# Order of the input loads and the sign step of the weight conversion in a fused retention, channel-mix and gated-MLP kernel on one core

## The chip, the cores and the metric

The kernel runs on one core of a Trainium2 chip. The metric is device time in microseconds, the median of several executions. Names of the engines: PE is TensorE (matmul), PEld its weight loads, DVE is VectorE, ACT is ScalarE, POOL is GpSimd, SP is SyncE, which here only issues DMAs.

## What is computed

Three layers on a batch of 2 with 768 steps and width 512. All arrays come in as float32; the host passes the weight matrices with their bytes viewed as 64-bit words of the kind that the kernel converts (below).

```python
def _attn_ref(q, k, v):                      # 8 heads of 64
    for t in range(S):
        state = gamma * state + einsum('bhd,bhe->bhde', k[:, :, t], v[:, :, t])
        y[:, :, t] = scale * einsum('bhd,bhde->bhe', q[:, :, t], state)

def _moe_ref(x, mu_k, mu_r, w_k, w_v, w_r):  # x_prev is x moved by one step
    xk = mu_k * x + (1.0 - mu_k) * x_prev
    xr = mu_r * x + (1.0 - mu_r) * x_prev
    k = np.maximum(xk @ w_k, 0.0)
    v = k * k @ w_v
    return sigmoid(xr @ w_r) * v

def _moe2_ref(x, w_in, g_ln, w_sg, b_sg, w_out):
    h = gelu_tanh(x @ w_in);  u, v = halves of h
    v_n = (v - mean(v)) / sqrt(var(v) + 1e-6) * g_ln
    v_s = einsum('ts,bsd->btd', w_sg, v_n) + b_sg[None, :, None]
    return x + (u * v_s) @ w_out
```

## The kernel before

**The chunk stage.** The retention runs over 12 chunks of 128 steps, numbered 0 to 11, the two batches in turn. A chunk has two loads of 512 KB each, `chunk<-qk` (queries and keys) and `chunk<-kv` (keys and values by token); I call them qk4, kv4 and so on. Its work on PE is `sc` (scores, L410), `y` from the state (L472, not for chunks 0 and 1), `st` (the state's update, L446, not for the last two chunks) and `y` from the scores (L483). POOL scales the values (`vs`, L424; for chunks 0 and 1 DVE does it), DVE masks the scores (`prs`, two operations to a chunk, L419) and, when both batches of a step range are through, scales `y` into `x` (two operations, L497). The state is copied from PSUM to `scr` by ACT or DVE (L241).

**The dense stage.** The rest are dense products of a 128-row weight block with 512 columns, each done as three passes (high part by high part, high by low, low by high) on fp32r pairs, 12 or 24 matmuls of 128x512 to an output tile, all issued at L322. Columns are in 3 blocks of 512. The order is: `kp` (x by w_k, 8 tiles) of block 0, a few `kp` tiles of block 1 ahead of time (EARLY of them), `rp` (w_r) and `vp` (w_v) of block 0, the same for blocks 1 and 2, then the MLP (`vp` and `up` by w_in, `sp` by w_sg, `op` by w_out). The input of a `kp` or `rp` product is made on DVE and ACT: `mix` (L521, L527), then the pair `xo` (a cast, and a subtraction at L311).

**Weights.** A weight piece (512 KB) is loaded into one of three `raw` buffers as 64-bit words. `convert` makes an fp32 value from two 32-bit halves: ACT scales the upper word (L267), ACT or DVE prepares the lower one (L275, L278), DVE joins them (L282, L285), DVE puts the sign bit in (L289), one of both casts the high part, and DVE subtracts for the low part (L293). There are 32 such pieces: 8 of w_k, 4 of w_r, 8 of w_v, 8 of w_in, 4 of w_out. The `kp` tile m needs w_k piece m.

**What sets the order.** The program builds a list of operations with costs, and `Plan.order` plays them through with a little model of the engines and of the DMA link; the order in which it starts them is the order of instructions on every engine. Pools limit it: `p4` has 17 slots, of which up to CHUNKS may hold chunk halves; `raw` has 3; `t` has 8 + EARLY. The chip then only waits for data, buffers and the landing of the DMA that is eight places earlier in SP's queue. All loads go through SP, in its order. w_k loads are let in once kv1 has landed in the model (`after=` in `raw_load`).

Of the kernel before, what the change touches and what calls it, by code (L numbers as in the profile page):

```python
# [35 lines left out]
WARM_UP = 10  # L36
EARLY = 5
CHUNKS = 6
XO = 4
DMA_SCRATCH = 4096  # L40
V_ON_POOL = tuple(range(2, 12))
LINK = 0.1
SLACK = {"raw": 2.0}
DMA_LEAD = 1.9
DMA_RATE = 0.40
F64_SIGN = -(1 << 31)
F64_REBIAS = 2.0 ** -112
# [4 lines left out]
class Plan:  # L52
# [28 lines left out]
    def order(self):  # L81
# [16 lines left out]
        engines = ("PE", "DVE", "ACT", "POOL", "SP")  # L98
        idle = {e: 0.0 for e in engines}
        queue = {e: [] for e in engines}  # L100
        seq, events, link = [], [(0.0, -1, e) for e in engines], 0.0
        started = [False] * n
# [30 lines left out]
        def start(i, t, eng):  # L133
# [14 lines left out]
            if eng == "SP":  # L148
                busy = t + 0.1
                link = max(t + DMA_LEAD, link + cost / DMA_RATE) if cost else link  # L150
                done = max(t + DMA_LEAD, link)
            else:
                busy = done = t + cost
# [43 lines left out]
def fused_kernel(ctx, tc, qk, kv, w_k, w_v, w_r, w_in, w_sg, w_out, consts, ydec, b_sg, out):  # L197
# [48 lines left out]
    def raw_load(key, src, dt, mb):  # L246
        buf = ("raw", key)
        plan.op("SP", mb, lambda: sp.dma_start(out=T[buf], in_=src), w=[(buf, 0)],
                new=[new("raw", "raw", buf, (128, src.shape[-1]), dt)],
                after=plan.writer[("kv", 1), 0])  # L250
        return buf

    def convert(name, j, src, dst, tag, part, first):
# [4 lines left out]
        def word(k):  # L258
            return T[raw].bitcast(I32).rearrange("p (n two) -> p n two", two=2)[:, :, k]

        def xf():
            return T[xb]

        def xi():
            return T[xb].bitcast(I32)

        plan.op("ACT", .68, lambda: act.activation(out=xf(), in_=word(1).bitcast(F32), func=ACTF.Copy,  # L267
                                                   scale=F64_REBIAS),
                r=[(raw, 0)], w=[(xb, 0)], new=[new_t("cv", xb)])
# [10 lines left out]
        def join():  # L280
# [7 lines left out]
        plan.op("DVE", .69, join, r=[(raw, 1)], w=[(xb, 0)])  # L288
        plan.op("DVE", .69, lambda: dve.scalar_tensor_tensor(  # L289
            out=xi(), in0=word(1), scalar=F64_SIGN, in1=xi(), op0=ALU.bitwise_and, op1=ALU.bitwise_or),  # L290
            r=[(raw, 0)], w=[(xb, 0)])
        cast(lambda: dst(T[wb][0]), lambda: T[xb], [(xb, 0)], [(wb, ("hi", part))], [first] if first else [])
# [544 lines left out]
```

## Time and profile before

| | before |
|---|---|
| median of 3 runs | 367.78 us (364.86 to 370.07) |
| profiled execution, its time | 369.48 us |
| span of the instructions in it | 367.4 us |
| PE busy | 354.3 us (96%) |
| DVE busy | 246.6 us (67%) |
| ACT busy | 155.4 us (42%) |
| POOL busy | 17.4 us (5%) |
| moved from and to HBM | 35.97 MB |

Times inside the profile count from the first instruction. The profiled execution took 2.1 us more than its span. A busy share is an average over stages: the shares of DVE and ACT are much higher in the first 120 us than later.

### The profile page before, as it was taken

How to read it: one execution, taken by the hardware profiler on the slowest of the kernel's cores; microseconds unless marked ns; L12 is line 12 of the kernel's file. 1: busy time of each engine (PE TensorE's matmuls, PEld its weight loads, DVE VectorE, ACT ScalarE, POOL GpSimd, SP SyncE). 2: the span in 40 equal slices, each digit the busy share in tenths (PEclk: the TensorE clock that was granted, in tenths of full speed). 3: DMA queues.
4: the chain of work that ended last, by engine and by line, in shares of the span. 5: the costliest groups of instructions: out<-in, count | busy, mean ns of one | idle time of the engine just before them, and what ended most of it. 6: DMA issues, size and time to landing. Idle time of an engine off the chain costs nothing.

```text
span 367.4 us, 5406 instructions
## 1 busy us (share of the span) xinstructions
PE 354.3 (96%) x2154; PEld 295.1 (80%) x2154; DVE 246.6 (67%) x481; ACT 155.4 (42%) x264; POOL 17.4 (5%) x19
## 2 busy tenths in 40 slices
PE   5959999999999999999999999999999999999995
PEld 2848888888888888888888888888888888899884
DVE  2779999899899895025899448669384666436422
ACT  1147538988998773006897034324133000000000
POOL 0334510000000000000000000000000000000000
PEclk9969999999999999999999999999999999999999
DMA  7999626114464025000133101110211000110032
GB/s 257 414 409 407 276 59 189 40 59 144 146 197 145 0 64 167 0 0 2 57 114 116 44 0 45 43 43 2 49 38 45 0 0 2 52 62 2 29 115 86
DMA packets 12136, 35.97 MB, mean 98 GB/s; under 512 B 1232, under 2 KB 3408, under 8 KB 12112
## 3 DMA queue, kind: packets, MB, share of 16 engines
q1 hardware_dynamic: 12112, 35.63, 28.6%
q8 instruction: 17, 0.28, 0.3%
q14 instruction: 7, 0.06, 0.1%
HBM read 32.48 MB, written 3.15 MB: 97 GB/s over the span
## 4 chain that ended last, share of the span: by engine, by line
PE 86%; DMA 7%; DVE 5%; SPq 1%; issue 0%
PE vp L322 27%; PE kp L322 18%; PE sp L322 14%; PE up L322 9%; PE rp L322 9%; PE op L322 7%; DMA chunk<-qk 3%; DMA scr<-ydec 2%; DVE prs L419 2%; DMA out<-o 2%; PE sc L410 1%; PE y L483 1%; DVE xo L311 1%; DVE o L732 1%; DVE mix L527 1%; DVE x L497 1%
## 5 line engine op out<-in xcount | busy, mean ns | idle before, releaser
L322 PE MATMUL kp<-xo,wk 128*128 128x512 f32 x288 | 66.5, 390 | 0.0
L322 PE MATMUL vp<-k,wv 128*128 128x512 f32 x288 | 65.8, 389 | 0.0
L322 PEld LDWEIGHTS kp<-xo,wk 128*128 128x128 f32 x288 | 53.8, 188 | 11.6 <-issue 0.5
L322 PEld LDWEIGHTS vp<-k,wv 128*128 128x128 f32 x288 | 54.1, 188 | 11.2
L322 PE MATMUL sp<-wsg,vh 128*128 128x512 f32 (+1 forms) x288 | 50.2, 336 | 0.0
L322 PEld LDWEIGHTS sp<-wsg,vh 128*128 128x128 f32 x288 | 44.4, 190 | 5.7
L322 PE MATMUL vp<-win,x2o 128*128 128x512 f32 x144 | 33.1, 389 | 0.0
L322 PE MATMUL up<-x2o,win 128*128 128x512 f32 x144 | 33.1, 389 | 0.0
L322 PE MATMUL rp<-xo,wr 128*128 128x512 f32 x144 | 33.1, 389 | 0.0
L322 PE MATMUL op<-gt,wout 128*128 128x512 f32 x144 | 33.0, 389 | 0.0
L322 PEld LDWEIGHTS vp<-win,x2o 128*128 128x128 f32 x144 | 27.0, 188 | 5.6
L322 PEld LDWEIGHTS up<-x2o,win 128*128 128x128 f32 x144 | 27.0, 188 | 5.6
L322 PEld LDWEIGHTS rp<-xo,wr 128*128 128x128 f32 x144 | 27.0, 188 | 5.6
L322 PEld LDWEIGHTS op<-gt,wout 128*128 128x128 f32 x144 | 27.0, 188 | 5.6
L566 DVE TENSOR_TENSOR x<-vp,x 128x512 f32<-128x512 f32 x12 | 8.3, 692 | 27.9 <-PE vp L322 27.9
L710 DVE SCALAR_TENSOR_TENSOR g<-sp,con,bsg 128x512 f32<-128x512 f32 x12 | 9.0, 752 | 23.4 <-PE sp L322 23.4
L267 ACT ACTIVATE cv<-raw 128x512 f32<-128x512 f32 x32 | 20.9, 668 | 6.5 <-DMA raw<-w_k 6.1
L289 DVE SCALAR_TENSOR_TENSOR cv<-raw,cv 128x512 int32<-128x512 int32 x32 | 22.1, 691 | 0.8
L547 ACT ACTIVATE k<-rk 128x512 fp32r<-128x512 f32 x19 | 12.0, 631 | 24.5 <-DVE rk L541 24.1
L732 DVE TENSOR_TENSOR o<-op,x 128x256 f32<-128x256 f32 (+1 forms) x20 | 8.8, 474 | 19.8 <-PE op L322 13.7
L410 PE MATMUL sc<-chunk 64*128 64x128 f32 x192 | 14.6, 296 | 7.8 <-DMA chunk<-qk 7.8
L410 PEld LDWEIGHTS sc<-chunk 64*128 64x128 f32 x192 | 12.4, 199 | 10.2 <-issue 6.1
(82 smaller groups left out, 416.9 us busy)
## 6 DMA issues: line engine op xcount, KB each, us to landing
chunk<-qk SPq DMA_DIRECT2D x12, 512.0 KB, 9.8
chunk<-kv SPq DMA_DIRECT2D x12, 512.0 KB, 10.1
raw<-w_k SPq DMA_DIRECT2D x8, 512.0 KB, 8.5
raw<-w_v SPq DMA_DIRECT2D x8, 512.0 KB, 3.5
raw<-w_in SPq DMA_DIRECT2D x8, 512.0 KB, 4.0
out<-o SPq DMA_DIRECT2D x12, 256.0 KB, 2.2
raw<-w_sg SPq DMA_DIRECT2D x6, 384.0 KB, 3.2
raw<-w_r SPq DMA_DIRECT2D x4, 512.0 KB, 4.1
```

The costliest lines, as they stand in the source:

```text
L267: plan.op("ACT", .68, lambda: act.activation(out=xf(), in_=word(1).bitcast(F32), func=ACTF.Copy, scale=F64_REBIAS), r=[(raw, 0)], w=[(xb, ...
L289: plan.op("DVE", .69, lambda: dve.scalar_tensor_tensor(out=xi(), in0=word(1), scalar=F64_SIGN, in1=xi(), op0=ALU.bitwise_and, op1=ALU.bitw ...
L311: plan.op("DVE", .69, lambda: dve.tensor_tensor(out=lo(), in0=src(), in1=hi(), op=ALU.subtract), r=[*keep, (buf, ("hi", part))], w=[(buf, ...
L322: pe.matmul(out=T[ps][:, cols], lhsT=l(), rhs=r(), start=first and q == 0 and i == 0, stop=q == 2 and i == len(grp) - 1, skip_group_check= ...
L410: pe.matmul(out=T["sc", i, p][:, j * CH:(j + 1) * CH], lhsT=a[par[p], 1, j], rhs=a[par[p], 0, j], start=j == 0, stop=j == KD - 1, skip_gro ...
L419: plan.op("DVE", .66, lambda p=p: dve.tensor_tensor(out=T["pr", i % 4][:, p], in0=heads(T["sc", i, p]), in1=T["mask"].unsqueeze(1).to_broa ...
L483: pe.matmul(out=y_at(i, j, p), lhsT=T["vs", i][:, 2 * j + p], rhs=T["pr", i % 4][:, p, j], start=c == 0 and b == 0 and j < 2, stop=b == B ...
L497: dve.tensor_tensor(out=T[x][:, e::2, :, 1 + off:1 + off + CH], in0=T["y", c, e].rearrange("p (b j t) -> p j b t", b=B, t=CH), in1=table[: ...
L547: plan.op("ACT", .63, lambda: act.activation(out=T[o][:, 0], in_=T[rk], func=ACTF.Square), r=[(rk, 0)], w=[(o, ("hi", 0))], new=[new_p("k2 ...
L566: plan.op("DVE", .69, lambda: dve.tensor_tensor(out=T[x2][:, m], in0=T[ps], in1=T[x2][:, m], op=ALU.mult), r=[(ps, 0)], w=[(x2, m)])
L710: dve.scalar_tensor_tensor(out=out_, in0=in_, scalar=T["vec"][:, 2, m:m + 1], in1=t.unsqueeze(1).to_broadcast([128, B, BW]) if last else t ...
L732: plan.op("DVE", .69 if g == B else .42, lambda n=n, ps=ps, o=o, m=m, part=part, of=of: dve.tensor_tensor(out=T[o][:, part], in0=T[ps][:, ...
```

## The change

Constants: eight chunk buffers for six, six early `kp` tiles for five (and so one more slot in `t`), and other numbers in the planner's model (start time, issue time, lead, tail and rate of the link). The w_k loads are let in two at a time, after the kv loads of chunks 4, 5, 6 and 7. In `convert` ACT's scaling uses Prelu with a negative scale and a slope of 2^-32 in place of Copy: a negative value comes out larger by 2^32 than a positive one of the same size, so that a bit of its exponent stands where the left shift by 3 in the join turns it into the sign; the DVE instruction that put in the sign bit is gone.

```diff
--- before.py
+++ after.py
@@ -34,16 +34,20 @@
 RSQRT_SEED = float(0x5F3759DF)
 PIECE = 512
 WARM_UP = 10
-EARLY = 5
-CHUNKS = 6
+EARLY = 6
+CHUNKS = 8
 XO = 4
+WK_AFTER = {("wk", j): k for j, k in enumerate((4, 4, 5, 5, 6, 6, 7, 7))}
 DMA_SCRATCH = 4096
 V_ON_POOL = tuple(range(2, 12))
 LINK = 0.1
 SLACK = {"raw": 2.0}
-DMA_LEAD = 1.9
-DMA_RATE = 0.40
-F64_SIGN = -(1 << 31)
+BEGIN = 0.75
+ISSUE = 0.4
+DMA_LEAD = 1.4
+DMA_TAIL = 2.0
+DMA_RATE = 0.41
+F64_SIGN = 2.0 ** 32
 F64_REBIAS = 2.0 ** -112
 F64_LOW_SCALE = 2.0 ** -29 * (1 - 2.0 ** -20)
 F64_LOW_BIAS = -0.4999
@@ -96,9 +100,9 @@
         home = {}
         pending = {}
         engines = ("PE", "DVE", "ACT", "POOL", "SP")
-        idle = {e: 0.0 for e in engines}
+        idle = {e: BEGIN for e in engines}
         queue = {e: [] for e in engines}
-        seq, events, link = [], [(0.0, -1, e) for e in engines], 0.0
+        seq, events, link = [], [(BEGIN, -1, e) for e in engines], 0.0
         started = [False] * n
 
         def put(i):
@@ -146,9 +150,10 @@
                 home[buf] = (pool, kind)
                 wait[pool].remove((i, kind))
             if eng == "SP":
-                busy = t + 0.1
-                link = max(t + DMA_LEAD, link + cost / DMA_RATE) if cost else link
-                done = max(t + DMA_LEAD, link)
+                busy = t + ISSUE
+                late = link > t + DMA_LEAD + 1.0
+                link = max(t + DMA_LEAD, link) + cost / DMA_RATE
+                done = link + (DMA_TAIL if late else 0.8)
             else:
                 busy = done = t + cost
             idle[eng] = busy
@@ -247,7 +252,7 @@
         buf = ("raw", key)
         plan.op("SP", mb, lambda: sp.dma_start(out=T[buf], in_=src), w=[(buf, 0)],
                 new=[new("raw", "raw", buf, (128, src.shape[-1]), dt)],
-                after=plan.writer[("kv", 1), 0])
+                after=plan.writer[("kv", WK_AFTER.get(key, 1)), 0])
         return buf
 
     def convert(name, j, src, dst, tag, part, first):
@@ -264,8 +269,8 @@
         def xi():
             return T[xb].bitcast(I32)
 
-        plan.op("ACT", .68, lambda: act.activation(out=xf(), in_=word(1).bitcast(F32), func=ACTF.Copy,
-                                                   scale=F64_REBIAS),
+        plan.op("ACT", .68, lambda: act.activation(out=xf(), in_=word(1).bitcast(F32), func=ACTF.Prelu,
+                                                   scale=-F64_REBIAS * F64_SIGN, alpha=1.0 / F64_SIGN),
                 r=[(raw, 0)], w=[(xb, 0)], new=[new_t("cv", xb)])
         by = []
 
@@ -286,9 +291,6 @@
                                          op1=ALU.bitwise_or)
         plan.op("DVE ACT", (.42, .68), lower, r=[(raw, 0)], w=[(raw, 1), (xb, 0)])
         plan.op("DVE", .69, join, r=[(raw, 1)], w=[(xb, 0)])
-        plan.op("DVE", .69, lambda: dve.scalar_tensor_tensor(
-            out=xi(), in0=word(1), scalar=F64_SIGN, in1=xi(), op0=ALU.bitwise_and, op1=ALU.bitwise_or),
-            r=[(raw, 0)], w=[(xb, 0)])
         cast(lambda: dst(T[wb][0]), lambda: T[xb], [(xb, 0)], [(wb, ("hi", part))], [first] if first else [])
         plan.op("DVE", .69, lambda: dve.tensor_tensor(out=dst(T[wb][1]), in0=T[xb], in1=dst(T[wb][0]),
                                                       op=ALU.subtract),
```

The lines of the changed kernel are two to five higher than before (PE's L322 is L324, the loads at L248 are L253, the join at L282 is L287).

SP's queue from the load of qk3 on, before. `raw` is a weight buffer, `chunk` a chunk half, and the number tells the buffer: chunk_150 is qk3, chunk_168 kv3, chunk_274 kv5.

```order
L351 DMA chunk_150<-qk 128x1024
L248 DMA raw_152<-w_k 128x512
L248 DMA raw_155<-w_k 128x512
L248 DMA raw_157<-w_k 128x512
L354 DMA chunk_168<-kv 128x1024
L351 DMA chunk_216<-qk 128x1024
L354 DMA chunk_240<-kv 128x1024
L351 DMA chunk_262<-qk 128x1024
L354 DMA chunk_274<-kv 128x1024
```

The same place in the changed kernel, where chunk_149 is qk3, chunk_152 kv3 and chunk_290 qk7.

```order
L353 DMA chunk_149<-qk 128x1024
L356 DMA chunk_152<-kv 128x1024
L353 DMA chunk_154<-qk 128x1024
L356 DMA chunk_179<-kv 128x1024
L353 DMA chunk_212<-qk 128x1024
L356 DMA chunk_228<-kv 128x1024
L353 DMA chunk_260<-qk 128x1024
L356 DMA chunk_271<-kv 128x1024
L353 DMA chunk_290<-qk 128x1024
L253 DMA raw_294<-w_k 128x512
L253 DMA raw_296<-w_k 128x512
L253 DMA raw_324<-w_k 128x512
```

kv3 now follows qk3 at once; the first three w_k loads moved from behind qk3 to behind qk7. The other five stand behind kv11, where before three of them stood among the chunk loads.

PE's queue at the end of the chunk stage, before: chunks 8 to 11 (x8 is one chunk's worth of matmuls).

```order
L472 MATMUL y<-chunk,scr_119 64x128 x8
L322 MATMUL kp<-xo,wk_284 128x512 x4
L410 MATMUL sc<-chunk 128x128 x8
L472 MATMUL y<-chunk,scr_119 64x128 x8
L446 MATMUL st<-vs,chunk 64x64 x8
L483 MATMUL y<-prs_147,vs 64x128 x8
L446 MATMUL st<-vs,chunk 64x64 x8
L483 MATMUL y<-prs_147,vs 64x128 x8
L410 MATMUL sc<-chunk 128x128 x16
L472 MATMUL y<-chunk,scr_118 64x128 x16
L322 MATMUL kp<-xo,wk_284 128x512 x4
L483 MATMUL y<-prs_148,vs 64x128 x16
```

And the same place in the changed kernel.

```order
L474 MATMUL y<-chunk,scr_129 64x128 x8
L412 MATMUL sc<-chunk 128x128 x8
L474 MATMUL y<-chunk,scr_129 64x128 x8
L448 MATMUL st<-vs,chunk 64x64 x8
L485 MATMUL y<-prs_137,vs 64x128 x8
L448 MATMUL st<-vs,chunk 64x64 x8
L485 MATMUL y<-prs_137,vs 64x128 x8
L412 MATMUL sc<-chunk 128x128 x16
L474 MATMUL y<-chunk,scr_128 64x128 x16
L324 MATMUL kp<-xo,wk_526 128x512 x4
L485 MATMUL y<-prs_138,vs 64x128 x16
```

Of the two groups of four `kp` matmuls that stood ahead of the last `y` one has moved behind it.

DVE's queue in the chunk stage, before, from the scores of chunk 3 to those of chunk 5; L282 is the join of a w_k piece, L289 its sign, L293 its low part.

```order
L419 TENSOR_TENSOR prs_148<-sc,con 128x512 x2
L282 SCALAR_TENSOR_TENSOR cv<-cv,raw 128x512
L289 SCALAR_TENSOR_TENSOR cv<-raw,cv 128x512
L282 SCALAR_TENSOR_TENSOR cv<-cv,raw 128x512
L289 SCALAR_TENSOR_TENSOR cv<-raw,cv 128x512
L293 TENSOR_TENSOR wk_285<-cv,wk_284 128x512
L282 SCALAR_TENSOR_TENSOR cv<-cv,raw 128x512
L293 TENSOR_TENSOR wk_285<-cv,wk_284 128x512
L419 TENSOR_TENSOR prs_147<-sc,con 128x512 x2
L289 SCALAR_TENSOR_TENSOR cv<-raw,cv 128x512
L497 TENSOR_TENSOR x<-y,scr_119 128x2x2x128 x2
L419 TENSOR_TENSOR prs_147<-sc,con 128x512 x2
```

And in the changed kernel, from the scores of chunk 3 to the first join (L287).

```order
L421 TENSOR_TENSOR prs_138<-sc,con 128x512 x2
L246 COPY scr_129<-st 128x512
L499 TENSOR_TENSOR x<-y,scr_129 128x2x2x128 x2
L421 TENSOR_TENSOR prs_137<-sc,con 128x512 x4
L529 SCALAR_TENSOR_TENSOR mix<-x,con,mix 128x512 x3
L499 TENSOR_TENSOR x<-y,scr_128 128x2x2x128 x2
L505 COPY x<-x 128x8
L421 TENSOR_TENSOR prs_138<-sc,con 128x512 x4
L313 TENSOR_TENSOR xo<-mix,xo 128x512 x3
L529 SCALAR_TENSOR_TENSOR mix<-x,con,mix 128x512
L287 SCALAR_TENSOR_TENSOR cv<-cv,raw 128x512
```

The joins moved from ahead of chunk 4's scores to behind chunk 7's, and no sign instruction is left between them.

Counted over the whole program DVE has 470 instructions for 483 (32 sign steps fewer, 19 others taken over from ACT), ACT 247 for 266 with three table loads in each, PE the same 1814 rows.

## Rows read from the trace of the kernel before

**Rows 1.** Who TensorE waited for, whole span: total us, times, longest

```profile
PE sc L410 <- DMA chunk<-qk: 7.8, 3, 4.1
```

**Rows 2.** The chain that ended last: start us, length us, what

```profile
51.05 1.12 PE kp L322 x4
52.17 1.94 PE y L483 x32
54.11 33.79 PE kp L322 x148
...
363.65 0.68 DVE o L732
```

**Rows 3.** Busy us (instructions) by stretch, granted clock, DMA share, GB/s

```profile
20.00:30.00 10.00, 7.11 (x96) 6.17 (x96) 7.66 (x11) 5.53 (x10) 4.41 (x4) 0.66 1.03 409
50.00:120.00 70.00, 70.00 (x359) 57.85 (x356) 64.64 (x106) 60.16 (x104) 0.00 (x0) 1.00 0.42 128
```

**Rows 4.** Timeline: start us, length us, engine; in brackets idle time and releaser

```profile
16.12 0.67 ACT L267 ACTIVATE cv<-raw 128x512 f32<-128x512 f32 x1 [1.32 <-DMA raw<-w_k]
...
19.09 0.66 ACT L267 ACTIVATE cv<-raw 128x512 f32<-128x512 f32 x1 [1.72 <-DMA raw<-w_k]
...
21.55 1.09 POOL L424 TENSOR_TENSOR vs<-chunk,con 128x512 f32<-128x512 f32 x1 [6.90 <-DMA chunk<-kv]
...
22.89 2.08 PE L410 MATMUL sc<-chunk 64*128 64x128 f32 x16 [4.07 <-DMA chunk<-qk]
...
24.11 1.18 POOL L424 TENSOR_TENSOR vs<-chunk,con 128x512 f32<-128x512 f32 x1 [1.47 <-DMA chunk<-kv]
...
26.67 1.09 POOL L424 TENSOR_TENSOR vs<-chunk,con 128x512 f32<-128x512 f32 x1 [1.38 <-DMA chunk<-kv]
```

**Rows 5.** Timeline, TensorE pieces of the chunk stage

```profile
9.12 1.16 PE L410 MATMUL sc<-chunk 64*128 64x128 f32 x16 [3.11 <-DMA chunk<-qk]
...
25.80 1.92 PE L483 MATMUL y<-prs,vs 128*64 128x128 f32 x16
...
28.36 1.16 PE L410 MATMUL sc<-chunk 64*128 64x128 f32 x16
...
30.05 0.69 PE L446 MATMUL st<-vs,chunk 128*64 128x64 f32 x16
...
32.88 1.16 PE L410 MATMUL sc<-chunk 64*128 64x128 f32 x16
...
36.26 0.69 PE L446 MATMUL st<-vs,chunk 128*64 128x64 f32 x16
```

**Rows 6.** Timeline, VectorE operations of the chunk stage

```profile
8.38 1.28 DVE L419 TENSOR_TENSOR prs<-sc,con 128x512 f32<-128x512 f32 x2
...
21.66 1.53 DVE L293 TENSOR_TENSOR wk<-cv,wk 128x512 fp32r<-128x512 f32 x1
...
23.71 0.68 DVE L293 TENSOR_TENSOR wk<-cv,wk 128x512 fp32r<-128x512 f32 x1
...
30.76 2.85 DVE L527 SCALAR_TENSOR_TENSOR mix<-x,con,mix 128x512 f32<-128x512 f32 x3
...
33.54 1.28 DVE L497 TENSOR_TENSOR x<-y,scr 128x512 f32<-128x512 f32 x2
...
38.67 1.74 DVE L311 TENSOR_TENSOR xo<-mix,xo 128x512 fp32r<-128x512 f32 x2
```

**Rows 7.** Page, groups of instructions: count, busy us, mean ns, idle before

```profile
L267 ACT ACTIVATE cv<-raw 128x512 f32<-128x512 f32 x32 | 20.9, 668 | 6.5 <-DMA raw<-w_k 6.1
L289 DVE SCALAR_TENSOR_TENSOR cv<-raw,cv 128x512 int32<-128x512 int32 x32 | 22.1, 691 | 0.8
L547 ACT ACTIVATE k<-rk 128x512 fp32r<-128x512 f32 x19 | 12.0, 631 | 24.5 <-DVE rk L541 24.1
```

**Rows 8.** Page, DMA issues: count, size, median us to landing

```profile
raw<-w_v SPq DMA_DIRECT2D x8, 512.0 KB, 3.5
```

## The prediction

> **What bounds the kernel now.** I read the chain of work that ended last first. From 54.11 us on it is TensorE's dense products, one behind the other, until only the last output tile is left [rows 2], and of all that TensorE waited for in the whole span, the one long item is `sc` for a chunk's qk load: 7.8 us in three waits, the longest 4.1 [rows 1]. All three lie in the chunk stage. So the time is the start of the unbroken dense stream, 54.11, plus what comes behind it, 367.40 - 54.11 = 313.29 us, which no instruction of this change makes shorter. The question is only how early the stream can start, and whether it stays fed.
>
> Why it starts at 54.11 is told by the timeline around 20 us. ACT gets the first w_k piece at 16.1 and the second at 19.1; POOL gets kv3 at 21.5, TensorE qk4 at 22.9, POOL kv4 at 24.1 and kv5 at 26.7 [rows 4]. Between kv4 and kv5 one more load lands, so a load of 512 KB takes 2.56 / 2 = 1.28 us of the link, and they land in the order of SP's queue: three w_k pieces stand there between qk3 and kv3. TensorE, through with chunk 2 at 22.89 - 4.07 = 18.8, idles for qk4. Behind that idle time its granted clock falls: 0.66 in the mean over 20 to 30 us [rows 3], with `sc` at 2.08 us for 1.16 and a `y` at 1.92 [rows 4, 5]. From the `sc` of chunk 5, 28.36, TensorE and VectorE then work almost without a pause.
>
> **The change part by part. The queue.** Each load is equally large, so I take a landing time as a slot and put the new order into the old slots. kv3 now has the slot of the first w_k piece, 16.1, and qk4 that of the second, 19.1. From there at 1.28 us each: qk5 is two loads later, 21.6; qk8 is eleven later (with three w_k pieces ahead of kv7), 33.2; kv11 is eighteen later, 42.1. The 2.97 us between the first two pieces, in place of 1.28, is a hiccup that I leave where it was.
>
> **TensorE's sum.** Until 18.8 I change nothing: `st` and `y` of chunk 0 now stand ahead of `sc` of chunk 1, and wait for `prs`, 8.38 + 1.28 = 9.66 [rows 6]; the `sc` that was done at 10.3 is done about 1.5 us later, but the stage then waits for qk2 in both orders. The prices at full clock: two `sc` with the two `y` from the state take 36.26 - 32.88 = 3.38, so 1.69 for a chunk; two `st` with their `y` take 32.88 - 30.05 = 2.83, so 1.415 [rows 5]; the last two `y` take 1.94, a group of four `kp` 1.12 [rows 2]. With kv3 and qk4 there in time, `st` and `y` of chunk 3 end at 18.8 + 1.4 = 20.2, and the `sc` of chunk 5 starts near 21.5 in place of 28.36. What is left from 20.2: 8 x 1.69 + 6 x 1.415 + 1.94 + 1.12 = 25.1, which ends at 45.3. But `sc` of chunk 8 is reached after 4 x 1.69 + 3 x 1.415 = 11.0, at 31.2, and qk8 lands at 33.2: a new stall of 2.0, and the end is **47.3**.
>
> **VectorE's sum.** It must not be later. From the end of chunk 3's `y`, 20.2, to the last `prs` its new order holds four pairs of `x` and eight of `prs` (12 x 1.28 = 15.4), four `mix` at 2.85 / 3 = 0.95 (3.8), four `xo` subtractions at 1.74 / 2 = 0.87 (3.5), two joins at 0.69 (1.4), one low part of w_k between 0.68 and 1.53 (1.1), and short copies (0.3) [rows 6, 7]: 25.5, so 45.7, and one `y` more, 46.7. The two engines are as good as level, and hand work to each other in turn. I add 0.6 us for that, my choice, with 0 and 2.5 as its ends: the stream starts at **47.9**.
>
> One group of four `kp` fewer is done ahead of the last `y`, so 1.12 us comes back behind it. The sum is 47.9 + 1.12 + 313.29 = 362.3 for the span, 5.1 less than 367.4.
>
> **The sign step.** 32 x 0.691 = 22.1 us of DVE work go [rows 7]. Two of them would lie in the sum above; the rest lies beside the dense stream, where TensorE waits for nothing, and is worth nothing by itself. If that cover were gone, it would be worth at most the 0.69 of a piece that is waited for. The planner gives DVE 19 other instructions from ACT, so both get lighter. A `raw` buffer comes free one DVE step earlier. **Prelu** is in no trace here. Below, the cheapest one-pass ACT row of this shape is 0.631, above, two passes of the Copy are 1.34; I take the Copy's 0.668, since it is one instruction on the same operands [rows 7].
>
> The Trainium skill, ScalarE: Activation LUTs (Step-by-step: what each stage is for), says that an ACTIVATE's cost per element is the same whatever the function; Copy and Square here, 0.668 and 0.631, agree but for a few per cent. By that rule Prelu changes nothing; it is one reason why I give its rival below little.
>
> **The weights behind the queue.** Five w_k pieces now stand behind kv11. The first of them needs a `raw` buffer, free at the first join (20.2 + 15 us of VectorE's list, about 36), and lands a slot behind kv11, at 43.4; `kp` tile 3 wants it at 47.9 + 1.8 + 2 x 2.74 = 55 (12 matmuls at 33.79 / 148 each [rows 2]). The sixth piece waits for the third join, which stands behind the last `prs`, so about 47; an unloaded link brings it in 3.5 [rows 8], and three ACT steps, one join and their turn make it about 57, wanted at 60.5. The last two follow with as much room. So I cost the move at nothing; its cover is some 3 us, and each us beyond that would be a us of stall. Six early tiles, a bigger `t` pool and the new planner numbers add no instruction to the path. The end of the program is in the same order as before.
>
> **Against which time.** On the profiled execution's own 369.48 the sum gives 364.4. The median of the runs shown, 367.78, is 1.7 lower, and with it the sum gives 362.7. I cannot tell whether the median execution had the hiccup and the slow clock in full, so I lean to the median without taking all of it: 363.2, about 1.3% less. A measurement of this kernel can tell about 2% from no change.
>
> **The rivals.**
>
> *The stream starves (0.15).* ACT was busy 60.2 and DVE 64.6 of the 70 us from 50 to 120 [rows 3]; a stream that starts 5 us earlier wants w_k, `xo` of block 1, w_r and w_v earlier. For it: these shares. Against it: both engines get lighter, and TensorE did not wait once there. It would give the gain back and end at 366 to 368.
>
> *The slow clock comes elsewhere (0.10).* An idle 3.11 us ahead of `sc` at 9.12 left that piece at 1.16 us, 4.07 did not leave the next at that [rows 4, 5]; the new order idles some 2.5 us at 6, and 2.0 at chunk 8. A half-clock stretch lengthens one `sc` and one `y` by 0.9 us each, and `st` and others by a few tenths: 2.2 us. Time 365.4.
> The Trainium skill, TensorE: Matmul & The Clock Gate (Part 1: The HAM clock gate), says that the throttled state is the default, that activity releases it, and that the moment varies from run to run; the rows agree with the first part, no run here shows the second.
>
> *Everything falls well (0.17).* No hiccup (TensorE's sum 1.7 shorter: 45.6), hand-offs free, low prices on VectorE (four `xo` and a low part at 0.68: 1.2 less, so 45.5): the stream starts at 45.6, 7.4 less than before with the 1.12 paid back. That gives 360.4, at the edge of 2%.
>
> *Slower (0.04).* Prelu is dear. ACT has 70 - 60.2 = 9.8 us to spare from 50 to 120, and converts 17 pieces there. At two passes that is 17 x 0.67 = 11.4 more, a stall of 1.6: 364.8. It decides from 375.1 on, 12 above my time: (12 + 9.8) / 17 = 1.28 us more for each, a Prelu of 1.95 us.
>
> **How the numbers follow.** The forecast has 0.54. Its own range is 47.3 to 49.8 for the start, on either base: 362 to 366. For 8 in 10 the range takes in the starved and slow-clock cases and half of the good one, 360.0 to 367.0. Faster by over 2% means under 360.4: the good case's better part, and a little from the forecast for the spread of the runs, 0.17 in all. Slower takes the last rival, 0.04. Within 2% is the rest, 0.79.
>
> **What would show it.** Right: TensorE's wait for qk4 gone, `sc` of chunk 5 at 21 to 22, no stretch of half clock near 21 to 28, a wait of 1 to 3 us at chunk 8 near 31, the dense stream unbroken from 47 to 50 on, the L272 group at 0.67 us. Wrong: a dense stream that starts by 50 but has waits for `wk`, `xo` or `wv` behind it (starved), `prs` as the releaser of many `y` (VectorE bound, hand-offs mis-sized), a granted clock under 1 in another stretch, or an L272 of over 1 us.

## The result

The changed kernel takes **362.86 us** (median of 4 runs, 362.21 to 364.01) where the kernel before takes 368.15 (4 runs, 364.86 to 370.07): a ratio of 0.987, with a 95% interval of 0.983 to 0.991. That is 1.3% faster, and so within 2%; the forecast was 363.2. The profiled execution took 363.22, with a span of 361.4. Of the ten runs of e5 below two (369.94, the profiled one, and 370.14) lie more than 1.5% above its fastest and are left out of its median, and the start of its stream is not given.

| | before | forecast | after |
|---|---|---|---|
| start of the unbroken dense stream, us | 54.11 | 47.9 | 47.25 |
| what comes behind it, to the end of the span | 313.3 | 314.4 | 314.2 |
| `sc` of chunk 5 | 28.36 | 21.5 | 21.5 |
| TensorE's waits for qk | 7.8 in three | 2.0 at chunk 8 | 1.0 at chunk 8 |
| first ACT step of a weight piece (32 of them) | 0.668 | 0.668 | 0.667 |

What comes behind is the span less the start: 361.4 - 47.25 = 314.2. First TensorE's waits over the whole span of the changed kernel (who waited for whom: total us, times, longest); it answers to [rows 1].

```profile
PE st L448 <- DVE vs L430: 1.7, 1, 1.7
PE warm L390 <- DVE x L494: 1.2, 1, 1.2
PE sc L412 <- DMA chunk<-qk: 1.0, 1, 1.0
PE y L474 <- ACT scr L246: 0.5, 1, 0.5
```

Of the three waits for qk one of 1.0 us is left. The list is complete: nothing in it is a `kp`, `rp` or `vp`, so the dense stream is not interrupted. Its chain (start us, length us, what) says the same, and answers to [rows 2]. It also shows what ended last ahead of the stream: VectorE's last `prs`.

```profile
43.72 2.40 DVE prs L421 x4
46.11 0.04 issue
46.16 1.09 PE y L485 x14
47.25 37.43 PE kp L324 x164
84.68 10.88 PE rp L324 x48
```

Then the stretches (us, and for PE, PEld, DVE, ACT and POOL the busy us with their instructions; granted clock, DMA share, GB/s), which answer to [rows 3].

```profile
0.00:20.00 20.00, 17.10 (x228) 12.55 (x230) 8.23 (x16) 1.87 (x2) 5.20 (x9) 0.91 0.90 346
20.00:30.00 10.00, 10.00 (x222) 9.07 (x220) 10.00 (x17) 7.43 (x13) 4.73 (x5) 1.00 1.03 408
30.00:40.00 10.00, 8.47 (x172) 7.40 (x169) 10.00 (x14) 4.94 (x9) 6.18 (x5) 1.00 1.01 399
40.00:50.00 10.00, 9.95 (x124) 8.03 (x121) 10.00 (x16) 5.46 (x10) 1.51 (x2) 1.00 0.37 112
50.00:120.00 70.00, 70.00 (x310) 57.95 (x310) 59.51 (x101) 56.38 (x99) 0.00 (x0) 1.00 0.41 130
```

The granted clock is 1.00 from 20 to 30 us, where it was 0.66. VectorE is busy 10.00 of 10 us in each of the three stretches of the chunk stage: it, not TensorE (8.47 from 30 to 40), is now the fuller engine there. From 50 to 120 it went from 64.64 to 59.51 busy, ACT from 60.16 to 56.38. One stretch of slower clock is new, early on (0.91 from 0 to 20). It is seen in TensorE's timeline (start us, length us, engine, operation; in brackets the idle time ahead and who ended it):

```profile
8.97 2.56 PE L485 MATMUL y<-prs,vs 128*64 128x128 f32 x16
...
11.47 2.39 PE L412 MATMUL sc<-chunk 64*128 64x128 f32 x32
...
20.47 2.06 PE L412 MATMUL sc<-chunk 64*128 64x128 f32 x32
...
31.93 1.16 PE L412 MATMUL sc<-chunk 64*128 64x128 f32 x16 [1.03 <-DMA chunk<-qk]
```

Sixteen `y` take 2.56 us at 8.97, where 1.05 is usual, and 32 `sc` take 2.39 at 11.47 for 2.06 at 20.47. The slow stretch took the place of the wait for qk2 that the forecast had there (the list above has none), and so hardly moved anything: the `y` of chunk 2 ended at 19.2, and 18.8 had been forecast.

The weight group of the profile's page, which answers to the first of [rows 7] (count, busy us, mean ns, idle before):

```profile
L272 ACT ACTIVATE cv<-raw 128x512 f32<-128x512 f32 x32 | 20.9, 667 | 0.0
```

### The profile page after: what moved, and what is told of

Read it like the earlier page. It is cut to its first block, busy times and chain, and to the rows that moved or that the text cites. A ratio compares the mean times of both kernels' runs of the same rounds, so it can differ in the third digit from the quotient of the medians.

```text
span 361.4 us, 5364 instructions
## 1 busy us (share of the span) xinstructions
PE 353.2 (98%) x2154; PEld 294.4 (81%) x2154; DVE 232.9 (64%) x468; ACT 143.3 (40%) x245; POOL 17.6 (5%) x19
## 3 DMA queue, kind: packets, MB, share of 16 engines
HBM read 32.48 MB, written 3.15 MB: 99 GB/s over the span
## 4 chain that ended last, share of the span: by engine, by line
PE 86%; DMA 10%; DVE 2%; issue 0%; SPq 0%
PE vp L324 27%; PE kp L324 18%; PE sp L324 14%; PE op L324 9%; PE up L324 9%; PE rp L324 9%; DMA chunk<-kv 4%; DMA raw<-w_k 3%; DMA chunk<-qk 3%; DVE prs L421 1%; DVE cv L287 0%; PE y L485 0%; DVE wk L295 0%; DVE x L499 0%; DVE o L734 0%
## 5 line engine op out<-in xcount | busy, mean ns | idle before, releaser
L324 PE MATMUL kp<-xo,wk 128*128 128x512 f32 x288 | 66.2, 390 | 0.0
L324 PE MATMUL vp<-k,wv 128*128 128x512 f32 x288 | 65.8, 389 | 0.0
L324 PEld LDWEIGHTS kp<-xo,wk 128*128 128x128 f32 x288 | 53.9, 188 | 11.5 <-issue 0.3
L324 PEld LDWEIGHTS vp<-k,wv 128*128 128x128 f32 x288 | 54.1, 188 | 11.2
L324 PE MATMUL sp<-wsg,vh 128*128 128x512 f32 (+1 forms) x288 | 50.2, 336 | 0.0
L324 PEld LDWEIGHTS sp<-wsg,vh 128*128 128x128 f32 x288 | 44.4, 190 | 5.7
L324 PE MATMUL rp<-xo,wr 128*128 128x512 f32 x144 | 33.1, 389 | 0.0
L324 PE MATMUL vp<-win,x2o 128*128 128x512 f32 x144 | 33.1, 389 | 0.0
L324 PE MATMUL up<-x2o,win 128*128 128x512 f32 x144 | 33.1, 389 | 0.0
L324 PE MATMUL op<-gt,wout 128*128 128x512 f32 x144 | 33.0, 389 | 0.0
L324 PEld LDWEIGHTS rp<-xo,wr 128*128 128x128 f32 x144 | 27.0, 188 | 5.6
L324 PEld LDWEIGHTS vp<-win,x2o 128*128 128x128 f32 x144 | 27.0, 188 | 5.6
L324 PEld LDWEIGHTS up<-x2o,win 128*128 128x128 f32 x144 | 27.0, 188 | 5.6
L324 PEld LDWEIGHTS op<-gt,wout 128*128 128x128 f32 x144 | 27.0, 188 | 5.6
L287 DVE SCALAR_TENSOR_TENSOR cv<-cv,raw 128x512 int32<-128x512 int32 x23 | 17.4, 758 | 1.3 <-ACT raw L280 1.3
L529 DVE SCALAR_TENSOR_TENSOR mix<-x,con,mix 128x512 f32<-128x512 f32 x24 | 18.1, 777 | 0.1
L552 DVE TENSOR_TENSOR k<-rk,k 128x512 fp32r<-128x512 f32 x18 | 12.4, 688 | 8.5 <-ACT rk L551 8.5
```

The lines of the kernel that those rows point to most:

```text
L287: dve.scalar_tensor_tensor(out=xi(), in0=xi(), scalar=3, in1=word(0), op0=ALU.logical_shift_left, op1=ALU.bitwise_or)
L324: pe.matmul(out=T[ps][:, cols], lhsT=l(), rhs=r(), start=first and q == 0 and i == 0, stop=q == 2 and i == len(grp) - 1, skip_group_check= ...
L529: plan.op("DVE", .75, lambda: dve.scalar_tensor_tensor(out=seg(T[f]), in0=T[x][:, kk, :, 1:BW + 1], scalar=T["vec"][:, i, kk:kk + 1], in1= ...
L552: plan.op("DVE", .69, lambda: dve.tensor_tensor(out=T[o][:, 1], in0=T[rk], in1=T[o][:, 0], op=ALU.subtract), r=[(rk, 0), (o, ("hi", 0))], ...
```

## The experiments

The theory after the result was the prediction's: the load order and the buffers that let it be (the **loads** half) bring the gain, and the shorter conversion (the **Prelu** half) lies under the dense stream and is worth little. The rival: VectorE has so little to spare behind an earlier stream that without the Prelu half the gain is lost. A third view gave part of the gain to the planner's new numbers. Ratios below are against the kernel before in the same session (its medians there: 368.14, 368.30 and 368.29). They are the record's, and not always the quotient of the two medians: for e7 that would be 0.985. The changed kernel was run in the first session alone, four times.

| kernel | median us (runs) | ratio, 95% | stream starts |
|---|---|---|---|
| the changed kernel | 362.86 (4) | 0.987, 0.983 to 0.991 | 47.25 |
| e1: after, with the sign step | 367.87 (10) | 0.999, 0.996 to 1.003 | 51.9 |
| e2: before, with Prelu alone | 366.75 (10) | 0.996, 0.993 to 1.000 | 51.08 |
| e3: before, with the loads alone | 367.22 (10) | 1.000, 0.996 to 1.003 | 47.01 |
| e10: before, with both, old planner | 362.76 (4) | 0.987, 0.981 to 0.994 | 45.84 |
| e8: after, sign step for w_k only | 366.18 (10) | 0.995, 0.992 to 0.998 | 46.44 |
| e9: after, sign step for the others | 363.81 (10) | 0.991, 0.987 to 0.994 | 47.17 |
| e4: after, w_k let in from the start | 364.26 (10) | 0.991, 0.987 to 0.994 | 48.65 |
| e5: after, six chunk buffers | 364.66 (8) | 0.992, 0.988 to 0.996 | |
| e7: after, w_k let in by chunks 7 to 10 | 362.71 (4) | 0.983, 0.979 to 0.987 | 47.47 |
| e12: e10, w_k spread over chunks 5 to 10 | 362.78 (6) | 0.987, 0.983 to 0.992 | 46.08 |
| e13: after, the same spread | 362.36 (6) | 0.987, 0.983 to 0.991 | 46.69 |
| e11: after, `vs` on ACT | 364.87 (10) | 0.994, 0.991 to 0.997 | 45.68 |

Most of these orders put one group of four `kp` (1.1 us) ahead of the start of the stream; before, e2 and e7 have two there, and e11 has none. Starts are to be compared with that in mind.

### The two halves apart

**e1**: the changed kernel with the conversion of before; the sign step stands inside the planner's entry of the join, so the order of all else is held.

```diff
-  func=ACTF.Prelu, scale=-F64_REBIAS * F64_SIGN, alpha=1.0 / F64_SIGN),
+  func=ACTF.Copy, scale=F64_REBIAS),
...
   # in join, behind its own instruction
+  dve.scalar_tensor_tensor(out=xi(), in0=word(1), scalar=F64_SIGN, in1=xi(),
+                           op0=ALU.bitwise_and, op1=ALU.bitwise_or)
```

> The changed kernel with Copy and the sign step back in the conversion, its order of all other instructions held as the changed kernel has it. Theory (the load order brings the gain, VectorE is full from 20 to 46 us of the chunk stage and free of consequence later): two sign steps lie ahead of the last prs, at 0.69 to 1.53 us each as the join there takes, so the dense stream starts 1.4 to 3.1 later than 47.25 and the time is 364.3 to 366.0; the 30 others cost nothing, TensorE waits for nothing behind 50 us. Rival A (the lighter conversion brings most of the gain): the time goes back to 367 to 368. Rival B (a raw buffer that is free one step earlier feeds the dense stream): waits of TensorE for wk, wr or wv behind 50 us.

Measured: 367.87, and the whole gain is gone: the time of rival A, with the waits of rival B. This is the miss that matters. TensorE's waits in e1 (as above; lines two on):

```profile
PE y L487 <- issue: 1.9, 1, 1.9
PE kp L326 <- DVE xo L246: 1.4, 1, 1.4
...
PE vp L326 <- ACT wv L246: 1.0, 1, 1.0
```

There are now 2.4 us of waits in the dense stream, for `xo` and for a converted piece of w_v. The stretches of e1, the first of them the 24 us from the start of its stream on, and then the same 24 us of the changed kernel:

```profile
51.91:75.91 24.00, 22.59 (x99) 18.42 (x99) 23.70 (x40) 19.58 (x35) 0.00 (x0) 1.00 0.42 132
50.00:120.00 70.00, 67.52 (x317) 55.18 (x313) 68.97 (x116) 54.78 (x96) 0.00 (x0) 1.00 0.42 129
```

```profile
47.25:71.25 24.00, 24.00 (x106) 19.85 (x107) 22.21 (x38) 21.69 (x39) 0.00 (x0) 1.00 0.41 132
```

VectorE is busy 23.70 of the 24 us for 22.21, and 68.97 of 70 from 50 to 120: it has next to nothing left. TensorE loses 2.5 us from 50 to 120, and ACT does 19.58 us of work in the 24 where the changed kernel's did 21.69. The profiled execution was a long one, 371.20: of its later start (51.9) 1.9 us are the pause of the first row above, which ended without a wait, and 1.6 the slower `sc` behind it (3.66 us for 32, against 2.06). By an estimate from these rows, without the 3.5 the start would be some 1.2 later than that of the changed kernel, and the waits and the matmuls behind the start add 3.3 (369.4 - 51.9 = 317.5, against 314.2): 4.5 together, near the 5.0 of the medians. So with the order of all else held the sign steps alone bring the old time back.

**e2**: the kernel before, order held, with the Prelu half alone (the sign entry of the plan stays and issues nothing).

```diff
-  func=ACTF.Copy, scale=F64_REBIAS),
+  func=ACTF.Prelu, scale=-F64_REBIAS * F64_SIGN, alpha=1.0 / F64_SIGN),
...
-  plan.op("DVE", .69, lambda: dve.scalar_tensor_tensor(
-      out=xi(), in0=word(1), scalar=F64_SIGN, in1=xi(), op0=..., op1=...), ...)
+  plan.op("DVE", .69, lambda: None, ...)
```

> The kernel before with Prelu and without the sign step, its order of all other instructions held. Theory (load order): the wait for qk4 near 19 to 23 us stays as it is, since the queue is the same; behind it VectorE's list loses two or three sign steps ahead of the last prs, so the stream starts at most 2 us earlier and the time is 366 to 368. Rival A (the lighter conversion): 363 to 364.

Measured: 366.75, 1.4 less than before, with the waits for qk as they were, 6.7 us in four. That lies in the range of the theory. By itself this half brings about a quarter of the gain, and its interval reaches to nothing.

**e3**: the kernel before with the loads half alone.

```diff
-CHUNKS = 6
+CHUNKS = 8
+WK_AFTER = {("wk", j): k for j, k in enumerate((4, 4, 5, 5, 6, 6, 7, 7))}
...
-  after=plan.writer[("kv", 1), 0])
+  after=plan.writer[("kv", WK_AFTER.get(key, 1)), 0])
```

> The kernel before with eight chunk buffers and the w_k loads let in between chunks 4 and 7; conversion, planner numbers and five early tiles as before. Theory (load order): no wait for qk4, sc of chunk 5 at 21 to 22 us, the sign steps still on VectorE's list, so the dense stream starts at 48.5 to 50.5 and the time is 364 to 366. Rival A (the lighter conversion): the wait goes, but the stream starts where it did, at 53 to 54, time 367 to 368.

Measured: 367.22, a ratio of 1.000: nothing that can be told is left. Neither expectation had this: the time is rival A's, but the stream does not start where it did. It starts at 47.01, 7.1 us earlier than before, and is then broken. TensorE's timeline of e3:

```profile
46.94 21.32 PE L323 MATMUL kp<-xo,wk 128*128 128x512 f32 x92
69.38 0.50 PE L323 MATMUL kp<-xo,wk 128*128 128x512 f32 x1 [1.12 <-DVE xo L242]
71.52 14.98 PE L323 MATMUL kp<-xo,wk 128*128 128x512 f32 x59 [1.64 <-DVE xo L242]
```

and VectorE's timeline shows where the `xo` was.

```profile
61.16 0.69 DVE L283 SCALAR_TENSOR_TENSOR cv<-cv,raw 128x512 int32<-128x512 int32 x1
61.88 0.69 DVE L290 SCALAR_TENSOR_TENSOR cv<-raw,cv 128x512 int32<-128x512 int32 x1
...
68.30 0.69 DVE L542 TENSOR_SCALAR rk<-kp 128x512 f32<-128x512 f32 x1 [1.39 <-PE kp L323]
68.91 0.42 DVE L242 CAST xo<-mix 128x512 fp32r<-128x512 f32 x1
...
71.04 0.42 DVE L242 CAST xo<-mix 128x512 fp32r<-128x512 f32 x1
```

TensorE wants `xo` of the next block from 68.3 on, and the casts of `xo` that it wants come at 68.91 and 71.04. What holds up the first is the order of VectorE's queue: ahead of it stands an `rk` that itself waits for TensorE's product, and VectorE stands idle for 1.39 us. So in this trace VectorE is not full at that place, and without the sign steps (L290) this order would have the same `rk` ahead of the cast. The planner laid the order for the longer conversion; that the longer conversion made it lay a worse one was not tested apart. Two waits cost 2.8; behind them 59 `kp` take 14.98 us, where 59 x 37.43 / 164 = 13.5 is the full-speed time, at a granted clock of 0.98 over 50 to 120 us. With the 1.1 for the one group of `kp` that is no longer ahead of the start, 7.1 - 1.1 - 2.8 - 1.5 = 1.7 are left of this execution's gain, and its span is 1.4 shorter (366.0).

**e10**: e3 with the Prelu half, and with the planner's numbers and the five early tiles of before.

```diff
 # e3, and
-  func=ACTF.Copy, scale=F64_REBIAS),
+  func=ACTF.Prelu, scale=-F64_REBIAS * F64_SIGN, alpha=1.0 / F64_SIGN),
...
-  plan.op("DVE", .69, lambda: dve.scalar_tensor_tensor( ... F64_SIGN ... ))
```

> The kernel before with eight buffers, the w_k loads let in between chunks 4 and 7, Prelu and no sign step, but with the old planner numbers and five early tiles. Second theory: this is both halves of the change, so it is as fast as the changed kernel, 362 to 364, stream start 47 to 48.5 and no wait behind it. Rival (the planner numbers or the sixth early tile keep the stream fed): the start is as early but TensorE waits 2 to 4 us for xo or wv behind it, 365 to 367.

Measured: 362.76. It is the changed kernel's time, so the planner's numbers and the sixth early tile bring nothing that can be told. Against e3 the only edit is the conversion, with the order that the planner then makes of all the rest, and the two are worth 367.22 - 362.76 = 4.5 us here. In this order VectorE casts `xo` at 59.58 and 61.26, and TensorE does not wait. The chain has one unbroken piece again:

```profile
45.84 34.72 PE kp L320 x152
```

**e8 and e9**: e1, with the sign step for the pieces of w_k alone, and for those of all other weights alone. Which pieces does VectorE have no time for?

```diff
   # e8; e9 has != for ==
+  how = dict(func=ACTF.Copy, scale=F64_REBIAS) if name == "wk" else dict(func=ACTF.Prelu, ...)
...
   # in join
+  if name == "wk":
+      dve.scalar_tensor_tensor(... the sign step ...)
```

> The changed kernel with Copy and the sign step back for the eight w_k pieces alone, order of all other instructions held. Second theory, formed after the first four runs (the load order sets the start of the dense stream, VectorE's spare time behind it sets whether the stream stays fed): two of these steps lie ahead of the last prs and six between 46 and 62 us, where VectorE also makes xo of block 1. So the stream starts 1.4 to 3 later than 47.25, and TensorE waits 0 to 2 us for xo at the first kp tile of block 1 near 70: 364.3 to 367. Rival (only the later pieces matter): as the changed kernel, 362 to 363.5.

> The changed kernel with Copy and the sign step back for the 24 pieces of w_r, w_v, w_in and w_out, order of all other instructions held. Second theory: the start stays at 47 to 48. VectorE was busy 59.5 of 70 us from 50 to 120 in the changed kernel; 12 sign steps there make 67.8, so it is just not full: waits for wr or wv of 0 to 2 us in all, 363 to 365. Rival (the later pieces carry the whole loss of e1): waits of 4 to 5 us behind 70, 367 to 368.

Measured: e8 366.18, 3.3 over the changed kernel, with eight sign steps; e9 363.81, 1.0 over it with twenty-four, which the intervals do not tell from it. Together 4.3, most of e1's 5.0. Both times lie in the ranges of the second theory, though the later start that it gave e8 is not there (46.44). VectorE's timeline of e8, and then that of the changed kernel, from the same join (the first of the two at 46.62) to the same cast of `xo`:

```profile
45.81 0.68 DVE L288 SCALAR_TENSOR_TENSOR cv<-cv,raw 128x512 int32<-128x512 int32 x1
...
59.90 0.69 DVE L294 SCALAR_TENSOR_TENSOR cv<-raw,cv 128x512 int32<-128x512 int32 x1
...
61.83 0.69 DVE L294 SCALAR_TENSOR_TENSOR cv<-raw,cv 128x512 int32<-128x512 int32 x1
...
69.12 0.42 DVE L246 CAST xo<-mix 128x512 fp32r<-128x512 f32 x1
```

```profile
46.62 1.28 DVE L287 SCALAR_TENSOR_TENSOR cv<-cv,raw 128x512 int32<-128x512 int32 x2
...
65.97 0.42 DVE L246 CAST xo<-mix 128x512 fp32r<-128x512 f32 x1
```

From the join to the cast VectorE's queue takes 69.12 - 45.81 = 23.31 us in e8 and 65.97 - 46.62 = 19.35 in the changed kernel. That is 3.96 more, nearly six sign steps of 0.69 in full, and e8 has six there (two of them shown). In the changed kernel the cast is done at 66.39, and TensorE needs it 95 `kp` matmuls behind the start, at 47.25 + 95 x 37.43 / 164 = 68.9: 2.5 us to spare. In e8 the cast starts 3.15 later and the stream 0.8 earlier, so it is late by 3.15 - 2.5 + 0.8 = 1.4. TensorE of e8 stands at that matmul from 68.2 on and waits just so long:

```profile
PE kp L328 <- DVE xo L246: 1.4, 1, 1.4
```

In e1 the same part of the queue takes 23.32 us (51.35 to 74.67), and the wait is 1.4 too. The execution of e8 in the trace took 364.10, 2.1 less than e8's median, and shows 1.4 of waiting and, from the start of its stream to the end of the block's `kp`, 39.1 us against 37.4. The rest of the 3.3 is not in this one trace.

### Where the w_k loads stand

**e4**: the changed kernel with w_k let in behind kv1, as before. **e5**: with six chunk buffers.

```diff
 # e4
-WK_AFTER = {("wk", j): k for j, k in enumerate((4, 4, 5, 5, 6, 6, 7, 7))}
+WK_AFTER = {}
 # e5
-CHUNKS = 8
+CHUNKS = 6
```

> The changed kernel with the w_k loads let in after kv1 again; with eight buffers the planner then puts two of them behind qk4 and one behind kv4, five loads earlier than in the changed kernel. Theory (landing order): qk5 comes three slots later, near 24 to 25, TensorE waits 2 to 3.5 us for it at chunk 5 and then not at chunk 8, so the stream starts 1 to 2 later, 363.5 to 365. Rival (VectorE's list alone sets the start): no change of the start beyond 0.5, 362 to 363.5.

> The changed kernel with six chunk buffers in place of eight, the w_k loads still let in between chunks 4 and 7. The planner then puts three of them behind qk5, four chunk halves earlier. Theory (landing order): kv5, qk6 and kv6 land three slots later, 26.7, 28.0 and 29.3, TensorE waits 1.5 to 3 us at chunks 5 and 6 in place of 1.0 at chunk 8; start of the dense stream 48 to 49.5, no wait behind it, 363.5 to 365. Rival (the number of buffers carries the gain by itself): the chip waits for buffers, start at 51 or later, 366 or more.

Measured: 364.26 and 364.66, 1.4 and 1.8 more than the changed kernel, both in the range of the theory, though each interval overlaps that of the changed kernel. In e4 the `sc` of chunk 5 is at 24.38, 2.9 later than in the changed kernel, behind a `vs` that POOL had late:

```profile
23.77 0.69 PE L448 MATMUL st<-vs,chunk 128*64 128x64 f32 x16 [1.74 <-POOL vs L426]
24.38 1.52 PE L412 MATMUL sc<-chunk 64*128 64x128 f32 x16
```

This is not the wait for qk5 that was expected: POOL had a `scr` step ahead of that `vs`, which waited for VectorE's `x` until 21.67. So the gate and the buffers may each be worth a part of the gain, which these runs do not settle, and most of it is there with either one taken back. The two were not taken back together.

**e7, e12, e13**: other gates. e7 lets w_k in later, e12 and e13 spread it one by one, so that fewer pieces stand ahead of qk8.

```diff
 # e7
+WK_AFTER = {("wk", j): k for j, k in enumerate((7, 7, 8, 8, 9, 9, 10, 10))}
 # e12 (on e10) and e13 (on after)
+WK_AFTER = {("wk", j): k for j, k in enumerate((5, 6, 7, 8, 8, 9, 9, 10))}
```

> The changed kernel with the w_k loads let in two at a time after the kv loads of chunks 7, 8, 9 and 10 in place of 4, 5, 6 and 7. Theory (VectorE's list ahead of the last prs sets the start of the dense stream): one join fewer stands there, qk8 has no weights ahead of it, so no wait at chunk 8; the stream starts at 45.2 to 46.2, and the time is 361 to 362. Rival (the w_k pieces come too late): waits for wk in the first kp tiles that give this back or more, 363 to 366.

> The kernel of e10 (old planner numbers, five early tiles) with the w_k loads let in one or two at a time after chunks 5, 6, 7, 8, 8, 9, 9, 10: one piece ahead of qk8 in place of three. Theory: the wait of 1.7 us for qk8 goes, VectorE's list loses a low part, the start of the dense stream is 45 to 46, no wait behind it; 361.5 to 362.5, against 362.76 for e10 and 362.86 for the changed kernel. Rival (later w_k pieces): waits for wk or xo, 363 to 365.

> The changed kernel with the same gate as e12. Theory: the wait of 1.0 us for qk8 goes, VectorE's list loses a low part, start 45.7 to 46.7, 361.5 to 362.5. Rival: waits for wk or xo behind the start as with the later gate of e7, 362.7 to 364.

Measured: 362.71, 362.78 and 362.36: none is to be told from the changed kernel, and e7 and e12 missed the ranges of their theory. The wait for qk8 is gone in all three traces, and something else comes in its place. In e7 and e13 it is a pause of TensorE that the profile puts down to no one, amid the `y` just ahead of the `sc` of chunk 8, and in e7 a late piece of w_k too:

```profile
PE y L485 <- issue: 1.1, 1, 1.1
PE kp L324 <- ACT wk L246: 0.7, 1, 0.7
```

In e12 it is a wait of 2.4 us for a qk near 9 us, with an `sc` at 2.07 us for 1.16 behind it. From the end of chunk 3's `y` to the start of the stream e12 takes 46.08 - 21.16 = 24.9 us, where e10, its parent, takes 45.84 - 19.46 = 26.4, with a wait of 1.7 for qk8 in it. So in that pair of traces the stage is 1.5 shorter without the wait, and the medians do not show it. Nor is VectorE full in all of them: in e13 it is busy 8.41 of the 10 us from 30 to 40, where it was busy 10.00 in the changed kernel. What the wait for qk8 is worth over many runs stays open.

### VectorE's dearer operations

**e11**: the joins took 1.53 us in the chunk stage of the changed kernel, for 0.68 later on. The suspect is POOL, which forms `vs` at the same time. Here ACT does it, head by head.

```diff
-  plan.op("POOL", 1.25, lambda: pool.tensor_tensor(out=T[vs], in0=T["kv", i][:, 1], in1=..., op=ALU.mult), ...)
+  def by_head():
+      for h in range(H):
+          act.mul(T[vs][:, h], T["kv", i][:, 1, h], T["vd"][:, c, h:h + 1])
+  plan.op("ACT", 2.6, by_head, ...)
```

> The changed kernel with vs of chunks 2 to 11 made by ACT, head by head, in place of POOL. In the changed kernel VectorE operations on two SBUF operands take 1.53 us beside a running vs of POOL and 0.68 without. Theory (POOL slows VectorE, and VectorE's list sets the start): joins, low parts and xo run at 0.68 to 0.75 in the chunk stage, the list ahead of the last prs is 2 to 4 us shorter, the start of the dense stream is then TensorE's, 45 to 46.5, time 360.5 to 362. Rival (ACT is too slow for it): st waits for vs of ACT, start at 48 or later, 363.5 or more; the durations still tell of the first part.

Measured: 364.87, slower than the changed kernel, as the rival said. The operations did become cheap (each `xo` subtraction of the stage 0.68 to 0.69), and the stream starts at 45.68, 1.6 earlier, of which 1.1 is the group of four `kp` that no longer stands ahead of it. But ACT works 21.91 us instead of 15.16 from 20 to 47, and the stream is then broken:

```profile
PE kp L324 <- DVE xo L246: 1.0, 1, 1.0
PE kp L324 <- ACT wk L246: 0.9, 2, 0.6
```

As in e3, an earlier start is not fed; here ACT has the more to do.

## Why the prediction came out

**The queue and the slots: right.** `sc` of chunk 5 was forecast near 21.5 and came there (the second half of the pair at 20.47), and the new stall came at chunk 8. The stall was 1.0 instead of 2.0. POOL had kv3 at 15.99, for a slot of 16.1, and kv4 at 19.12, for 20.4: the hiccup of the link was smaller by 1.3 in this execution, and all loads behind it came so much earlier, qk8 at 31.9 instead of 33.2. The five w_k pieces behind kv11 made no wait, as forecast.

**The two sums: right in total, the allowance wrong.** TensorE's sum gave 47.3 and VectorE's 46.7; the stream starts at 47.25. That TensorE's sum meets it is luck, for two errors cancel: qk8 came 1.3 earlier, and from there to the start it took 47.25 - 31.93 = 15.3 us, where the sum has 47.3 - 33.2 = 14.1. TensorE waited 0.5 for `scr`, and its last 32 `y`, behind VectorE's `prs`, took 2.58 us for 1.94. It is VectorE's list that set the start. The 0.6 for hand-offs was too much. VectorE's list had the joins too cheap (1.53 each, for 0.69) and the rest a little too dear, and its last `prs` ended at 46.1, where 45.7 was forecast.

**What comes behind, and the base: right.** 314.2 against 314.4, the group of `kp` that moved behind included. The sum gave 5.1 us of gain; the two medians differ by 5.3, the two profiled executions by 369.48 - 363.22 = 6.3, since that of before was a long one of its kind.

**Prelu: right.** 0.667 against 0.668, on either side of the edit one instruction over the same operands. The Trainium skill, ScalarE: Activation LUTs (Step-by-step: what each stage is for), gives all functions one cost per element; this row now shows it for Prelu.

**The slow clock: the place wrong, no cost.** The half-clock stretch near 21 to 28 is gone as forecast. Another came near 9 (the rival gave 0.10 to one there or at chunk 8, for 2.2 us), in the time of the wait for qk2, and made 0.4 of it.

**The step that failed: "The sign step".** The prediction said that what lies beside the dense stream "is worth nothing by itself", and that with the cover gone it "would be worth at most the 0.69 of a piece that is waited for". The cover was read from the kernel before, where TensorE waits for nothing behind 54. It does not hold once the stream starts at 47. There the sign steps are worth 5.0 us with the order held (e1), and 4.5 with the order planned anew (e3 against e10); with them the loads half brings nothing that can be told (e1, e3). The bound of 0.69 was wrong because the sign steps stand in one queue with the `xo` that the stream needs: each delays all that stands behind it, six of them lengthen the queue ahead of an `xo` cast by 3.96 us (e8), and only 2.5 were to spare. That accounts for a wait of 1.4 in the one trace; what makes up the rest of e8's 3.3 stays open. That the time came out right owes something to luck: the sum takes a fed stream for granted, and what kept it fed is the removal that was put at nothing. The rival "the stream starves" (0.15) named the mechanism; "both engines get lighter", which I put against it, is what kept it off. It is no by-product: without it the gain is gone (e1), as 366.75 - 362.86 = 3.9 us of it are without the loads (e2; the planner's numbers, which e2 lacks too, bring nothing by e10).

So the gain of 5.3 is no sum of two parts: e2 has 1.4 and e3 nothing that can be told, together they have all. The loads make the start early, and the lighter VectorE lets it count.

## What to carry to other kernels

When a change both starts a stage earlier and removes work that lay hidden behind it, price the removed work in the new schedule: add up the queue of each feeding engine from the new start to the first thing that the stage needs from it, and compare it with that time (here 2.5 us were to spare, for six steps of 0.69). Work that is removed from the queue of one engine can be worth what it delays in sum, not the length of one piece. Look also at the order: an operation that waits for the busy engine (the `rk` of e3) holds up what that engine needs next, if it stands ahead of it. For reordered loads of one size the spacing held well: kv4 to kv11 took 40.82 - 19.12 = 21.7 us for 17 loads, 1.28 each. The hiccup that had been carried over from the old trace put the whole row 1.3 late.

## What the runs showed of the hardware

**VectorE beside POOL.** In the changed kernel the operations of VectorE with two operands in SBUF take up to 1.53 us when a `vs` of POOL runs, and 0.68 without; those with an operand in PSUM (`prs`, `x`) keep their price. VectorE's timeline, then POOL's:

```profile
33.16 0.74 DVE L529 SCALAR_TENSOR_TENSOR mix<-x,con,mix 128x512 f32<-128x512 f32 x1
33.82 1.53 DVE L287 SCALAR_TENSOR_TENSOR cv<-cv,raw 128x512 int32<-128x512 int32 x1
35.27 1.27 DVE L421 TENSOR_TENSOR prs<-sc,con 128x512 f32<-128x512 f32 x2
...
38.86 0.68 DVE L313 TENSOR_TENSOR xo<-mix,xo 128x512 fp32r<-128x512 f32 x1
39.46 1.53 DVE L295 TENSOR_TENSOR wk<-cv,wk 128x512 fp32r<-128x512 f32 x1
40.91 1.53 DVE L287 SCALAR_TENSOR_TENSOR cv<-cv,raw 128x512 int32<-128x512 int32 x1
...
46.03 0.68 DVE L295 TENSOR_TENSOR wk<-cv,wk 128x512 fp32r<-128x512 f32 x1
```

```profile
33.21 1.59 POOL L426 TENSOR_TENSOR vs<-chunk,con 128x512 f32<-128x512 f32 x1 [1.12 <-PE sc L412]
...
35.79 1.04 POOL L426 TENSOR_TENSOR vs<-chunk,con 128x512 f32<-128x512 f32 x1 [0.99 <-DMA chunk<-kv]
...
38.88 1.56 POOL L426 TENSOR_TENSOR vs<-chunk,con 128x512 f32<-128x512 f32 x1
40.82 1.07 POOL L426 TENSOR_TENSOR vs<-chunk,con 128x512 f32<-128x512 f32 x1 [0.38 <-DMA chunk<-kv]
```

POOL's operation grows as well, from 1.04 to 1.56 and 1.59. The rows look like two engines that take turns. POOL's operations of 33.21, 38.88 and 40.82 each end 0.90 us after the VectorE operation that ran when they began (the `mix` of 33.16, the `xo` of 38.86, the `wk` of 39.46), and the VectorE operations of 33.82, 39.46 and 40.91 each end 0.55 after POOL's. With `vs` taken off POOL (e11) one VectorE operation of 1.53 is left in the stage, the `mix` at 29.28, and beside it the one POOL operation that is long, 1.43 at 28.84. The Trainium skill, GPSIMD Engine Reference (1. Specifications), says that its SBUF interfaces are shared with VectorE and contended by VectorE instructions with two SBUF inputs; the rows agree. The price here is up to 0.85 us for an operation of this size, and less where POOL's is nearly through: an `xo` of e10 took 0.86 us.

**Pauses without a wait.** In e1, e7 and e13 TensorE stands still for 1.9, 1.1 and 1.1 us amid the `y` of the chunk stage, ended by "issue", so by nothing that the profile shows. All three lie between 26 and 33 us, when chunk loads still land, and e5's trace has one of 1.9 from 25.3 on. A late packet of the queue that brings instructions does not tell them apart: between 29.6 and 30.0 us there is one in e7, with its pause, and one in e12, which has none. What causes the pauses stays open; nothing was tried.

**A short wait can cost twice.** In e3 two waits of 1.1 and 1.6 us in the dense stream were followed by 1.5 us of slower matmuls, at a mean granted clock of 0.98 over the 70 us, and in e1 the pause of 1.9 was followed by 16 `y` at 1.09 and then by 32 `sc` at 3.66 for 2.06. The wait of 1.0 at chunk 8 of the changed kernel was not: the `sc` behind it took 1.16, the full-clock time. The Trainium skill, TensorE: Matmul & The Clock Gate (Part 1: The HAM clock gate), says that the throttled state is the default and that activity releases the throttle; slower matmuls behind idle time agree with it, and these rows show that not every wait brings them.
